# A planned attention and state-space kernel: a planner that counts semaphore waits, more plans to choose from, and eleven more slots for exp results

## The chip, the cores and the metric

The kernel runs on one core of a Trainium2 chip. The metric is the time of one execution on the device in microseconds (us). The engines of the core are TensorE (PE in the profile; PEld are its weight loads), VectorE (DVE), ScalarE (ACT), GpSimd (POOL) and SyncE (SP), which issues most of the DMAs. Each engine has its own stream of instructions in a fixed order, and they wait for one another by semaphores.

## What is computed

Two independent parts, whose outputs lie side by side. Part A is a state-space layer over 2048 steps with 640 states. Part B is attention with 32 heads that share one key and one value head, over 2048 positions.

```python
def _A_ref(x, Lambda_re, Lambda_im, B_re, B_im, C_re, C_im, log_dt, Dskip):
    ...                                   # Lam_bar, B_bar from Lambda, log_dt, B
    Bu = jnp.einsum("bld,pd->blp", x + 0j, B_bar)
    for t in range(L):
        h = Lam_bar[None, :] * h + Bu[:, t, :]
        hs.append(h)
    return 2.0 * jnp.einsum("blp,dp->bld", hseq, Cmat).real + x * Dskip[None, None, :]

def _B_ref(x, wq, wk, wv, wo):            # S = 2048, D = 640, H = 32, Dh = 20
    q = ...                               # x @ wq, in 32 heads
    k, v = x @ wk, x @ wv                 # one head
    p = _softmax(jnp.einsum("bhqd,bkd->bhqk", q, k) * (Dh ** -0.5))
    o = jnp.einsum("bhqk,bkd->bhqd", p, v)
    return ... @ wo
```

The exponentials are the bulk: 32 heads x 2048 x 2048. The kernel cuts them into 2048 tiles of 128 keys x 512 queries; 64 tiles are a block (four heads, 512 queries, all keys).

## The kernel before

The kernel is not written instruction by instruction. A planner runs when it is built: operations with an engine, a planned duration, dependencies and a priority go through a small event model of the engines, and whichever operation an engine would take next is appended to the program. The order is fixed then. On the chip nothing of the plan's times is left; only the order of each engine and the semaphore waits are.

```python
class Schedule:
    OUT = {"pe": 200.0, "act": 130.0, "dve": 110.0, "pool": 150.0, "dma": 60.0}  # ns until another engine sees a result
    ...
    def begin(self, op, eng):
        ...
        if op.dma_key is not None:
            self.free[eng] = self.t + op.tail * len(op.fns)
            ...
        else:
            op.end = self.t + op.dur + op.tail
            self.free[eng] = self.t + op.dur - (self.EARLIER.get(eng, 0.0) if op.psum else 0.0)
        self.order.append(op)
```

Several plans are made, with task times shaken by a seed, and the one whose last operation ends first in the model is kept:

```python
    PLANS = 24
    def planned(self):
        for seed in range(self.PLANS):
            ...
            plan.s.run()
            end = max(op.end for op in plan.s.order)
            if best is None or end < best[0]:
                best = (end, plan)
```

A tile of scores is made by one matmul from KT and QT into one of eight 512-column PSUM banks. There are two ways from scores to exponentials.

The ScalarE way: one ACTIVATE turns two or three banks at once (SC0 or SC1, 1024 or 1536 columns) into bf16 in slots of PR, and one matmul for each tile multiplies it by the values (VP), accumulating in the bank MB3. There are 24 slots:

```python
    NPT = 24
    def fill(self, op, i):
        ...
        h = self.pr_take(n)
        ...
        dst = p.PR[:, h.index:h.index + n, :]
        ex = self.act(lambda e: e.activation(dst, t[:, 0:512 * n], ACT.Exp, scale=1.0 / UNIT), 0.8333 * 512 * n + 64, ...,
                      gate=lambda: all(x.taken and x.left == 0 and self.s.done(x.users) for x in h.prev))
```

The VectorE way: a first step adds a constant to the scores and writes integers whose bits are a coarse bf16 exponential; three more copies with other shifts (VectorE or GpSimd, two tiles at a time) are made from it; all four are multiplied by scaled values (VS) and summed by TensorE, so such a tile costs four matmuls. The results are the slots DR: 20 of their own at first and 21 more (MORE) once the space of x, wq and QP, all in one tensor BIG, is no longer needed.

```python
    NDS = 20
    MORE = 21
        first = self.dve(self.ts(self.dr(h.index), bank.ap, 16256.0, 0.0, ALU.add, ALU.max), 645, ...)   # in fill_d
            op.fns.append(self.ts(at(dst), at(src), float(self.SHIFTS[k][0]), 0.0, ALU.add, ALU.max))    # in copy
```

How many tiles go which way is not fixed: up to a share of 0.265 a tile goes the VectorE way whenever a bank, enough free DR slots and VectorE's state in the model allow it. All other tasks (projections of q, the state-space units, the output products) are fitted between.

At the start TensorE runs dummy matmuls on zeros while it has nothing else, so that its clock is up when work comes; the planner takes them for 260 ns each. When work runs low later, short dummy matmuls (KT, VZ) do the same.

```python
    def warm_source(self):
        ...
        return Op("pe", [self.mm(self.pvbank.ap, p.PR[:, 0, 0:128], p.PR[:, 0, :], True, True)], 260.0, prio=9, ...)
```

In the profile L1218 is the ACTIVATE of exps, L652 the additions of the VectorE way, L647 among others GpSimd's copies, L637 and L633 the matmuls.

Of the kernel before, what the change touches and what calls it, by code (L numbers as in the profile page):

```python
# [22 lines left out]
class Op:  # L23


    __slots__ = ("eng", "fns", "dur", "deps", "prio", "reads", "writes", "prev", "gate", "hook", "start", "end",
                 "seq", "land", "dma_key", "idx", "tail", "mode", "load", "late", "port", "after", "due", "table", "psum")

    def __init__(self, eng, fns, dur, deps=(), prio=5, reads=(), writes=(), prev=None, gate=None, hook=None,
                 dma_key=None, land=0.0, tail=0.0, mode="F", load=0.0, port=False):  # L30
        self.eng, self.fns, self.dur = eng, list(fns), dur
        self.deps, self.prio, self.prev = list(deps), prio, prev
        self.reads, self.writes = list(reads), list(writes)
        self.gate, self.hook = gate, hook
        self.dma_key, self.land, self.tail = dma_key, land, tail
        self.mode, self.load, self.late = mode, load, False
        self.port, self.after, self.due, self.table = port, [], None, None
        self.psum = any(k[0] == "B" and k[1:].isdigit() for k in self.reads)
        self.start = self.end = None
        self.seq = self.idx = 0  # L40


class Schedule:
# [3 lines left out]


    ENGINES = ("pe", "act", "dve", "pool", "sp")
    OUT = {"pe": 200.0, "act": 130.0, "dve": 110.0, "pool": 150.0, "dma": 60.0}  # L50
    OWN = {"pe": 0.0, "act": 60.0, "dve": 115.0, "pool": 100.0}
    URGENT = 1.0

# [8 lines left out]
    def __init__(self, seed=0):  # L62
        self.rng = random.Random(seed) if seed else None
        self.t = 0.0
        self.pending = {e: [] for e in self.ENGINES}
        self.free = {e: 0.0 for e in self.ENGINES}
        self.order = []
        self.events = []
        self.procs = []
        self.dma_free = {}  # L70
        self.n = 0
        self.mode = None
        self.late_from = 0.0
        self.loads = []
        self.sources = {e: [] for e in self.ENGINES}
        self.slack = {"pe": 60.0, "dve": 150.0}
        self.port_free = {"dve": 0.0, "pool": 0.0}
        self.port_last = {"dve": None, "pool": None}
        self.port_wanted = False
        self.pipe, self.table = 0.0, None  # L80

    def recent(self, span):

# [44 lines left out]
    def begin(self, op, eng):  # L128
        if op.hook is not None:
            op.hook(op)  # L130
        op.start = self.t
        if op.late:
            self.late_from = self.t + op.dur + self.PAUSE
        if eng == "pe":
            if op.mode != self.mode:
                op.dur += self.SWITCH
                self.mode = op.mode
            self.loads.append((self.t, op.load))
        if op.port:
            if eng == "pool" and self.port_last["dve"] is not None:  # L140
                op.after.append(self.port_last["dve"])
            self.port_free[eng] = self.t + op.dur + (self.LOCK if eng == "pool" else 0.0)
            self.port_last[eng] = op
            self.at(self.port_free[eng])
        if op.dma_key is not None:
            self.free[eng] = self.t + op.tail * len(op.fns)
            s = max(self.t + 1300.0, self.dma_free.get(eng, 0.0), self.pipe)
            self.dma_free[eng] = self.pipe = s + op.dur
            op.end = max(s + op.dur + 700.0, self.free[eng] + 1700.0) + op.land
        else:  # L150
            if op.table is not None and op.table != self.table:
                self.table = op.table
                op.dur += self.TABLE
            op.end = self.t + op.dur + op.tail
            self.free[eng] = self.t + op.dur - (self.EARLIER.get(eng, 0.0) if op.psum else 0.0)
        self.order.append(op)
        self.at(self.free[eng])
        for lag in (0.0, 60.0, 100.0, 110.0, 115.0, 130.0, 150.0, 200.0):
            self.at(op.end + lag)

    stay = staticmethod(lambda: True)

# [252 lines left out]
class Build:  # L415
# [3 lines left out]
    NOP = 7  # L419
    NRD = 3  # L420
    NDS = 20
    MORE = 21
    SHARE = 0.265

    SHIFTS = ((0, 0.2421875), (32, 0.201171875), (64, 0.169921875), (96, 0.142578125))
# [13 lines left out]
    def build(self):  # L439
        nc = self.nc  # L440
        with ExitStack() as o:
            self.banks = []
            self.slots = []
            sizes = list(self.CHUNKS) + [1] * (8 - sum(self.CHUNKS))
            self.psum = [o.enter_context(nc.psum_tensor(f"{'SC' if i < len(self.CHUNKS) else 'MB'}{i}", [128, 512 * n], FP32))
                         for i, n in enumerate(sizes)]
            self.alloc(o)
            base = nc.sbuf_bytes_remaining
            with ExitStack() as p1:
                self.alloc_early(p1)  # L450
                early = base - nc.sbuf_bytes_remaining
            with ExitStack() as p2:
                self.alloc_late(p2)
                late = base - nc.sbuf_bytes_remaining
                if late < early:
                    self.sb(p2, "pad", [128, (early - late) // 4 + 8], FP32)
                plan = self.planned()
                shares = {k: self.EARLY for k in self.LATE}
                shares.update({k: self.EARLY for k in ("pb0", "pb1", "lb", "qt")})
                shares.update({f"W{c}_0": self.EARLY + ["pb0", "pb1"] for c in range(NC)})  # L460
                shares.update({f"W{c}_1": self.EARLY + ["lb", "qt", "pc0", "pc1"] for c in range(NC)})
                shares.update({"pc0": ["lb"], "pc1": ["qt"]})
                shares.update({f"CB{c}": [f"xbT{i}_{k}" for i in range(2) for k in range(NC)] for c in range(NC)})
                shares.update({f"CT{tb}_{c}": [f"xn{tb}"] for tb in range(2) for c in range(NC)})
                shares.update({f"DR{self.NDS + i}": over for i, over in enumerate(self.dr_over)})
                shares["WOt"] = [f"BT{i}_{c}" for i in range(2) for c in range(NC)]
                shares.update({f"OPT{k}": [f"BA{i}_{c}" for i in range(2) for c in range(NC)] for k in self.EARLY_O})
                em = Emitter(nc, plan.s.order, [b.key for b in plan.banks], shares)
                em.plan()
                with nc.Block() as block:  # L470
                    em.emit(block)
# [15 lines left out]
        self.early = [b for b in self.banks if b not in rest]  # L487

    SPREAD = 12.0
    PLANS = 24  # L490

    def planned(self):

        best = None
        for seed in range(self.PLANS):
# [3 lines left out]
            try:  # L499
                plan.s.run()  # L500
            except RuntimeError:
                continue
            end = max(op.end for op in plan.s.order)
            if best is None or end < best[0]:
                best = (end, plan)
        return best[1]
# [1 line left out]
    def alloc(self, o):  # L508
# [9 lines left out]
        for c in range(NC):  # L518
            for m in range(2):
                self.dr_at.append(2048 * c + 640 + 512 * m)  # L520
                self.dr_over.append([f"xbT{i}_{c}" for i in (1, 2, 3)])
        for m in range(6):
            self.dr_at.append(ends[0] + 512 * m)
            self.dr_over.append(["wqa", "wqb"])
        for m in range(NC):
            self.dr_at.append(ends[1] + 512 * m)
            self.dr_over.append([f"QP{m}"])
        self.xaT = sb(o, "xaT", [128, NC, 2, 512], BF16)
        self.BT = sb(o, "BT", [128, 2, NC, 640], BF16)
        self.BA = sb(o, "BA", [128, 2, NC, 640], BF16)  # L530
# [124 lines left out]
    def program(self):  # L655
# [9 lines left out]
        self.q_op, self.qd_op, self.half_op, self.scat_op, self.rd_op, self.brow_op = {}, {}, {}, {}, {}, {}  # L665
        self.o_ops, self.y_ops, self.w_op, self.xa_op = {}, {}, {}, {}
        self.state_op = {}
        self.owner = [None] * self.NPT
        self.pr_at = 0
        self.waiting = []  # L670
        self.dhold = [Holder(i) for i in range(self.NDS)]
# [28 lines left out]
    def warm_source(self):  # L700
# [4 lines left out]
        if self.started:  # L705
            if self.s.recent(3000.0) > self.WARM:
# [1 line left out]
            fns = self.four(self.pvbank, [p.VZ[:]] * 4, p.KT[:, 0:512], True, True)  # L708
            return Op("pe", fns, self.mmt(512), prio=3.5, mode="C", load=512.0, reads=["VZ", "KT0"], writes=[self.pvbank.key],
                      deps=[self.c_op["VZ"], self.kt_op[0]])  # L710
        return Op("pe", [self.mm(self.pvbank.ap, p.PR[:, 0, 0:128], p.PR[:, 0, :], True, True)], 260.0, prio=9,
                  load=512.0, deps=[self.zero_op], reads=["PR0"], writes=[self.pvbank.key], hook=self.warm_last)

    WARM = 4500.0
    V_AT, BOUND_AT = (-88, -87), -99

# [467 lines left out]
    def fill(self, op, i):  # L1184
# [16 lines left out]
        ents = []  # L1201
        for x, m in enumerate(tiles):
            b, kc, j = self.score(op, m, t[:, 512 * x:512 * x + 512], banks[x])
            ents.append((b, kc, j, p.PR[:, h.index + x, :]))
        first = [] if own is None else [self.fill_d(op, own, banks[2])]
        if first:
            other = self.slot_last[1 - i][0]
# [6 lines left out]
        op.reads = sorted(set(op.reads))  # L1214
        op.dur = self.mmt(512, len(op.fns))
        op.load = 128.0 * len(op.fns)
        dst = p.PR[:, h.index:h.index + n, :]
        ex = self.act(lambda e: e.activation(dst, t[:, 0:512 * n], ACT.Exp, scale=1.0 / UNIT),  # L1218
                      0.8333 * 512 * n + 64, table="exp",
                      deps=[op], reads=[b.key for b in banks[:n]], writes=keys, prio=0.5,  # L1220
# [32 lines left out]
        return h  # L1253

    def pr_next(self, n):
        return self.pr_at if self.pr_at + n <= self.NPT else 0

    def tight(self):

# [171 lines left out]
    def more(self):  # L1431

        yield lambda: NQB - 1 in self.row_mm and self.s.done([self.row_mm[NQB - 1]]) \
            and all(self.s.done([self.qd_op[NQB - 1, i]]) for i in range(NC))
        self.dhold += [Holder(self.NDS + i) for i in range(self.MORE)]

    def d_free(self):

# [865 lines left out]
```

## Time and profile before

| | |
|---|---|
| median of 3 runs | 745.45 us (744.23 to 745.55) |
| span of the profiled execution | 743.5 us |
| exps on ScalarE | 676 instructions, 475 of two tiles and 201 of three: 1553 tiles |
| first steps of the VectorE way | 456 from SC banks and 39 from MB banks: 495 tiles |
| GpSimd copies | 401 |

The page has the busy time of each engine, the span in 40 slices with the busy share of each in tenths, and the chain of waits followed back from the last instruction. A group line has the engine, the operation, output and input, shape and count; then its busy time and the mean duration of one, then the idle time of the engine before it and who ended it. Busy time counts overlaps of following instructions once, the mean does not. A timeline line merges instructions that follow each other on an engine: start, length, engine, line, the shape of the first, and how many.

### The profile page before, as it was taken

What the parts mean: (1) busy time and instruction counts of PE and PEld (TensorE: products, weight loads), DVE (VectorE), ACT (ScalarE), POOL (GpSimd) and SP (SyncE); (2) the same over time, 40 slices, a digit from 0 to 9 for tenths busy, and PEclk for the clock granted to TensorE, in tenths of its full rate; (3) what the DMA queues carried; (4) which work ended last, traced back from release to release, by engine and by line L of the source; (5) the groups of instructions that cost most, each with busy time, mean ns of one, the idle gap of its engine ahead of it and who ended that gap; (6) DMA issues with size and microseconds to landing.
All of it is one profiled execution on the core that took longest, in us unless ns stands there. A gap on an engine that the chain in (4) does not pass through costs nothing.

```text
span 743.5 us, 26647 instructions
## 1 busy us (share of the span) xinstructions
PE 711.7 (96%) x11323; PEld 255.9 (34%) x11323; DVE 665.3 (89%) x1367; ACT 722.9 (97%) x702; POOL 426.3 (57%) x448
## 2 busy tenths in 40 slices
PE   9999899998999999999999999989999999999997
PEld 3422222234443533332333333323333333332332
DVE  6888999989788798999898999998998998988995
ACT  5999999999999999999999999999999999999995
POOL 3766566430266558367476674566754835778460
PEclk9999999999999999999999999998999999999999
DMA  9414443364220100101100000110000011100101
GB/s 200 70 41 129 91 113 90 89 144 78 48 60 10 25 20 21 51 11 35 42 26 23 17 30 19 40 46 19 19 14 19 9 27 30 37 16 17 26 14 37
DMA packets 78089, 34.43 MB, mean 46 GB/s; under 512 B 58852, under 2 KB 77972, under 8 KB 77972
## 3 DMA queue, kind: packets, MB, share of 16 engines
q1 hardware_dynamic: 76352, 32.34, 18.3%
q8 instruction: 90, 1.47, 0.8%
q10 hardware_dynamic: 1620, 0.39, 0.3%
q14 instruction: 27, 0.22, 0.1%
HBM read 11.53 MB, written 9.75 MB: 29 GB/s over the span
## 4 chain that ended last, share of the span: by engine, by line
ACT 59%; PE 34%; DVE 6%; issue 1%; DVEq 0%
ACT PR L1218 59%; PE MB L637 12%; PE SC L637 11%; PE MB L633 10%; DVE BIG L652 2%; DVE prod L647 1%; DVE W L652 1%; DVE CT L647 1%; DVE CA L647 1%; DVE g L2046 0%; PE SC L633 0%; DVE pvsb L1580 0%; DVE CT L651 0%; DVE CA L651 0%; PE SC L935 0%
## 5 line engine op out<-in xcount | busy, mean ns | idle before, releaser
L1218 ACT ACTIVATE PR<-SC 128x1024 bf16<-128x1024 f32 (+1 forms) x676 | 708.6, 1252 | 3.3 <-PE SC L637 2.1
L647 POOL TENSOR_TENSOR BIG<-BIG,step 128x512 int32<-128x512 int32 x401 | 407.4, 1045 | 286.1 <-DVE BIG L652 163.1
L652 DVE TENSOR_SCALAR BIG<-SC 128x512 int16<-128x512 f32 x456 | 302.8, 684 | 38.5 <-PE SC L637 34.9
L637 PE MATMUL SC<-QT,KT 32*128 32x512 bf16 x2009 | 265.3, 386 | 23.0 <-ACT PR L1218 16.0
L637 PE MATMUL MB<-BIG,VS 128*32 128x512 bf16 x1980 | 248.5, 386 | 1.2 <-issue 0.6
L637 PE MATMUL MB<-PR,VP 128*32 128x512 bf16 x1553 | 217.4, 386 | 0.8 <-DVE pvsb L1580 0.6
L637 PEld LDWEIGHTS SC<-QT,KT 32*128 32x128 bf16 x2009 | 67.8, 91 | 258.2 <-ACT PR L1218 165.3
L652 DVE TENSOR_SCALAR BIG<-BIG 128x1024 int16<-128x1024 int16 (+1 forms) x356 | 129.0, 419 | 8.6 <-PE MB L637 7.0
L637 PEld LDWEIGHTS MB<-BIG,VS 128*32 128x32 bf16 x1980 | 62.6, 95 | 66.7 <-issue 44.1
L637 PEld LDWEIGHTS MB<-PR,VP 128*32 128x32 bf16 x1553 | 53.5, 94 | 54.6 <-issue 41.0
L633 PE MATMUL MB<-CT,W 128*32 128x320 bf16 (+2 forms) x1040 | 49.7, 301 | 0.2 <-DVE BIG L2006 0.2
L633 PE MATMUL MB<-xaT,BT 128*32 128x256 bf16 x800 | 34.5, 274 | 0.0
L633 PE MATMUL MB<-xaT,BA 128*32 128x256 bf16 x800 | 33.6, 274 | 0.1
L633 PE MATMUL MB<-CA,W 128*32 128x512 bf16 (+1 forms) x640 | 31.2, 301 | 0.1
L647 DVE TENSOR_TENSOR prod<-MB,tab 128x1024 bf16<-128x1024 f32 x20 | 24.3, 1215 | 3.7 <-PE MB L633 3.7
L652 DVE TENSOR_SCALAR BIG<-MB 128x512 int16<-128x512 f32 x39 | 26.5, 680 | 1.1 <-PE MB L637 0.7
L633 PEld LDWEIGHTS MB<-CT,W 128*32 128x32 bf16 x1040 | 21.4, 96 | 17.0 <-issue 7.9
L633 PE MATMUL MB<-WO,OP 128*32 128x128 bf16 (+1 forms) x576 | 26.5, 297 | 0.1
L1761 DVE CAST stg<-MB 128x512 bf16<-128x512 f32 x35 | 23.9, 683 | 2.6 <-PE MB L633 2.3
L633 PE MATMUL MB<-BIG 128*32 128x512 bf16 x340 | 25.6, 383 | 0.0
L2046 DVE TENSOR_TENSOR_SCAN g<-sc,hst,prod 128x256 bf16<-128x256 f32 x30 | 23.1, 776 | 0.0
L633 PEld LDWEIGHTS MB<-xaT,BA 128*32 128x32 bf16 x800 | 19.0, 96 | 9.0 <-issue 5.4
(167 smaller groups left out, 421.2 us busy)
## 6 DMA issues: line engine op xcount, KB each, us to landing
out_dram<-stg SPq DMA_DIRECT2D x31, 128.0 KB, 1.7
qd<-BIG SPq DMA_DIRECT2D x20, 128.0 KB, 1.8
QT<-qd SPq DMA_DIRECT2D x28, 80.0 KB
OP<-pvsb SPq DMA_DIRECT2D x105, 20.0 KB
rdP<-recs SPq DMA_DIRECT2D x105, 20.0 KB
W<-in_A_B_re_dram SPq DMA_DIRECT2D x10, 160.0 KB, 2.7
W<-in_A_B_im_dram SPq DMA_DIRECT2D x10, 160.0 KB, 2.7
lbd<-W SPq DMA_DIRECT2D x10, 160.0 KB, 2.0
```

The lines of the kernel that those rows point to most:

```text
L633: r = e.matmul(out[32 * j:32 * j + 32], lhsT=lhsT[:, 32 * j:32 * j + 32], rhs=rhs, start=start, stop=stop, tile_position=(0, 32 * j), skip ...
L637: return lambda e: e.matmul(out, lhsT=lhsT, rhs=rhs, start=start, stop=stop, **kw)
L647: return lambda e: e.tensor_tensor(out, a, b, op)
L652: return lambda e: e.tensor_scalar(out, a, s1, s2, op0=op0, op1=op1)
L1218: ex = self.act(lambda e: e.activation(dst, t[:, 0:512 * n], ACT.Exp, scale=1.0 / UNIT), 0.8333 * 512 * n + 64, table="exp", deps=[op], re ...
L1761: ev = self.dve(lambda e: e.tensor_copy(st, bank.ap), 645, deps=[prev], reads=[bank.key], writes=[key], prio=self.EV, gate=(lambda: last.e ...
L2046: o = self.dve(lambda e, ri=ri, init=init: e.tensor_tensor_scan(p.g[:, u, ri, :], rdec, p.prod[:, 1, 0, ri, :], init, ALU.mult, ALU.add), ...
```

## The change

Four things. (1) In the planner's model an operation that starts before its inputs are seen by the engine keeps the engine until they are; until now waits that the emitted program has, but that the planner's list of dependencies lacked (a buffer to be read before it is overwritten, a bank that another engine reads), took no time in the model. A result of ScalarE is seen after 225 ns instead of 130. A cold dummy matmul is planned at 450 ns. (2) Each finished plan is replayed in order, with each operation starting when its engine is free and all that it waits for is seen (215 ns after TensorE), and the plan with the earliest end of that replay is kept. (3) 40 plans instead of 24. (4) The last eleven of the 21 late slots of the VectorE way become slots for exps ("wide"), so that there are 35 late on instead of 24, and 30 slots for the VectorE way instead of 41.

```diff
-    OUT = {"pe": 200.0, "act": 130.0, "dve": 110.0, "pool": 150.0, "dma": 60.0}
+    OUT = {"pe": 200.0, "act": 225.0, "dve": 110.0, "pool": 150.0, "dma": 60.0}
+    SEEN = {"pe": 215.0, "act": 225.0, "dve": 110.0, "pool": 150.0, "dma": 60.0}
...
+    def stall(self, op):
+        eng, late = op.eng, self.t
+        found = list(op.after)
+        for k in op.reads:
+            if k in self.writer:
+                found.append(self.writer[k])
+            if k[0] == "B" and k[1:].isdigit():
+                found += [x for x in self.readers.get(k, ()) if x.eng != eng]
+        for k in op.writes:
+            if k in self.writer:
+                found.append(self.writer[k])
+            found += self.readers.get(k, ())
+        op.found = [d for d in found if d is not op and (eng != "pe" or d.eng != "pe")]
+        for d in op.found:
+            late = max(late, self.seen(d, eng))
+        ...
+        return late - self.t
...
+        wait = self.stall(op)
+        if wait > 0.0:
+            if op.dma_key is None:
+                op.dur += wait
+                op.stall = wait
...
+    def replayed(self):
+        ...
+        for op in self.order:
+            e = op.eng
+            t = free[e]
+            for d in op.found:
+                out = self.SEEN["dma"] if d.dma_key is not None else self.OWN.get(e, 0.0) if d.eng == e else self.SEEN[d.eng]
+                t = max(t, end[id(d)] + out)
+            dur = op.dur - op.stall
+            ...
+        return max(end.values())
...
-    MORE = 21
+    MORE = 10
...
-    PLANS = 24
+    PLANS = 40
...
-            end = max(op.end for op in plan.s.order)
+            end = plan.s.replayed()
...
-        for m in range(6):
-            self.dr_at.append(ends[0] + 512 * m)
-            self.dr_over.append(["wqa", "wqb"])
-        for m in range(NC):
-            self.dr_at.append(ends[1] + 512 * m)
-            self.dr_over.append([f"QP{m}"])
+        self.wide_at = [(self.NPT, 6, ends[0]), (self.NPT + 6, NC, ends[1])]
+        self.pr_over = [["wqa", "wqb"]] * 6 + [[f"QP{m}"] for m in range(NC)]
...
-        return Op("pe", [...], 260.0, prio=9,
+        return Op("pe", [...], self.COLD if self.s.t < self.WARMED else 240.0, prio=9,
...
+    COLD, WARMED = 450.0, 6000.0
...
-        dst = p.PR[:, h.index:h.index + n, :]
+        dst = self.pr(h.index, n)
...
     def pr_next(self, n):
-        return self.pr_at if self.pr_at + n <= self.NPT else 0
+        ends = [self.NPT] + ([at + k for at, k, _ in self.wide_at] if self.wide else [])
+        ...
...
         self.dhold += [Holder(self.NDS + i) for i in range(self.MORE)]
+        self.wide = True
```

## The prediction

> **What bounds the kernel now.** I read the page first, for the share of each engine:
>
> ```profile
> PE 711.7 (96%) x11323; PEld 255.9 (34%) x11323; DVE 665.3 (89%) x1367; ACT 722.9 (97%) x702; POOL 426.3 (57%) x448
> ACT  5999999999999999999999999999999999999995
> PEclk9999999999999999999999999998999999999999
> ACT 59%; PE 34%; DVE 6%; issue 1%; DVEq 0%
> ```
>
> ScalarE (ACT) is busy 97% of the span, and the two slices in which it is not are the first and the last. The chain of waits leaves ScalarE for 41% of the span, but that alone doesn't say that ScalarE waits: a chain also goes through a matmul that ended just as the exp before it did. So I asked how fast exps can follow each other. The groups by shape give the counts, the timeline of ScalarE gives stretches that are nearly of one shape (start, length, engine, line, form of the first, count of all):
>
> ```profile
> L1218 ACT ACTIVATE PR<-SC 128x1024 bf16<-128x1024 f32 x475 | 447.9, 1112 | 2.0 <-PE SC L637 1.4
> L1218 ACT ACTIVATE PR<-SC 128x1536 bf16<-128x1536 f32 x201 | 277.9, 1585 | 1.3 <-PE SC L637 0.7 <-PE MB L637 0.4
> ```
>
> ```profile
> 152.67 39.65 ACT L1218 ACTIVATE PR<-SC 128x1024 bf16<-128x1024 f32 x30
> ...
> 659.53 28.48 ACT L1218 ACTIVATE PR<-SC 128x1536 bf16<-128x1536 f32 x30
> ...
> 324.76 1.02 ACT L1218 ACTIVATE PR<-SC 128x1024 bf16<-128x1024 f32 x1 [0.29 <-PE SC L637]
> ...
> 733.23 1.19 ACT L1218 ACTIVATE PR<-SC 128x1024 bf16<-128x1024 f32 x1
> ```
>
> In the trace's records the first stretch is 2 exps of two tiles and 28 of three (all of three from 153.58), the second the reverse. The means 1112 and 1585 ns overlap from one exp to the next, so they are not costs. Call S and L what a two-tile and a three-tile exp add. The exp that stands alone took 1.02, some 0.1 over S, so a stretch has 0.1 of latency: 2S + 28L = 39.55 and 28S + 2L = 28.38. The difference gives L - S = 11.17/26 = 0.430, the sum L + S = 67.93/30 = 2.264: **S = 0.917 us, L = 1.347 us**, and a tile more costs 0.430.
>
> All exps of the kernel before then need 475 x 0.917 + 201 x 1.347 = 435.6 + 270.7 = 706.3 us. They run from 23.02 to 734.42 (733.23 + 1.19), which is 711.4. So the kernel before is **23.0 us of start, 706.3 us of exp work, 5.1 us of stalls between exps, and 9.1 us of tail**. That sum is what the change can act on. Everything else is hidden behind ScalarE.
>
> **What the Trainium skill says.** "ScalarE: Activation LUTs", section "What ACT_TABLE_LOAD costs", gives 186 ns + 0.833 ns per element for an ACTIVATE and some 93 ns of overlap with the next; an estimate from it is 0.946 us for 1024 elements and 1.373 us for 1536. The trace agrees on the slope (0.430 us for 512 elements against 0.427) and is about 30 ns lower on the fixed part; I take the trace. "Perfetto Trace Analysis", section "Identifying the Most-Contended Engine", says that matmul busy time is no measure of how near TensorE is to its limit and that for ScalarE occupancy is. This trace agrees: PE shows 96% with weight loads at 34%, and exps still follow each other nearly without a gap. "TensorE: Matmul & The Clock Gate", Part 1, says that a 512-column matmul takes 426.7 ns while the array is cold and 215.7 ns once warm; nine warm-up matmuls that end just before 9.4 (below) stand 0.216 apart, and the first five near 0.43, so the trace agrees. That is what the new figure COLD = 450 is for.
>
> **The change part by part.**
>
> (1) *The planner charges waits to the engine.* An operation whose inputs aren't seen yet keeps its engine for that long, and a result of ScalarE is seen after 225 ns instead of 130. No duration on the chip changes; what changes is the order, and with it how many tiles go the VectorE way. Counted in the two programs: the VectorE way makes 482 tiles instead of 495 (first steps 428 + 54 against 456 + 39; matmuls with VS 1928 against 1980, four per tile). ScalarE therefore makes 1566 tiles instead of 1553, in 448 two-tile exps, 223 three-tile ones and one of a single tile. With S and L: 448 x 0.917 + 223 x 1.347 + 0.49 (S less 0.430) = 410.8 + 300.4 + 0.5 = 711.7, against 706.3: **+5.4 us on the bounding engine**. The 13 fewer first steps at the 684 ns of that group give VectorE some 9 us, GpSimd has 21 fewer copies; neither is the bound, so this pays only through fewer stalls.
>
> (2) *Fewer warm-up matmuls at the start.* The timeline of TensorE, before:
>
> ```profile
> 5.83 0.19 PE L637 MATMUL MB<-ident,vrow 20*128 20x20 bf16 x1
> 5.96 1.03 PE L637 MATMUL MB<-PR 128*128 128x512 bf16 x2
> 6.92 0.62 PE L637 MATMUL MB<-PR,VZ 128*32 128x512 bf16 x4
> 7.47 2.12 PE L637 MATMUL MB<-PR 128*128 128x512 bf16 x9
> 9.44 1.06 PE L637 MATMUL SC<-ident,CT 128*128 128x128 bf16 x16
> 10.51 0.40 PE L637 MATMUL MB<-BIG 128*20 128x512 bf16 x4
> ```
>
> The first part of x (read as CT) had landed at 6.06 by its semaphore, the second at 8.61, yet the transposes began at 9.44: they stood behind warm-up matmuls that were planned at 260 ns and took some 430 while cold. The new program has 3 + 2 + 1 + 6 of them ahead of the transposes instead of 5 + 4 + 2 + 9, eight fewer. The transposes can begin about 1.9 us earlier. But the four matmuls after them need the first part of wq, which landed at 9.33, so only 10.51 - 9.45 = 1.06 us get through, and later steps (table tiles on ScalarE before its exp table load, five warm-ups instead of three before the bound) eat some of it. I take **-0.8 us** for the first exp.
>
> (3) *40 plans instead of 24, judged by an in-order replay with 215 ns after TensorE, and eleven slots more for exps* (24 + 11, ten instead of 21 spare slots for VectorE's tiles). This acts on the 5.1 us of stalls and on nothing else in the middle. The stalls come in knots; the largest, by the chain of waits and the windows:
>
> ```profile
> 494.51 4.33 DVE BIG L652 x11
> 498.85 0.66 DVE g L2046
> 499.51 1.18 DVE BIG L652 x2
> ...
> 500.00:600.00 100.00, 95.28 (x1602) 35.91 (x1606) 91.67 (x176) 98.71 (x95) 62.50 (x62) 0.97 0.07 18
> ```
>
> At the end of a block TensorE waited for eleven copies of VectorE, its granted clock then halved for 6.8 us (0.97 in that window), and ScalarE stood. More room for exps lets the next block go on meanwhile, and a VectorE with 13 tiles less reaches the end of a block sooner. I expect two thirds of the stalls to go: **-3.3 us**.
>
> (4) *The tail.* The new program's last VectorE steps are 9 copies after the last bank copy but one, with twelve keep-warm matmuls among the last attention matmuls; before it was similar with none. **+0.3 us**.
>
> Sum: 5.4 - 0.8 - 3.3 + 0.3 = +1.6 us on 745.45: **747.0 us**.
>
> **The rivals.**
> *Stalls were larger than the page shows, and the new model removes them.* If the 41% of the chain off ScalarE were true waiting, a faithful plan could win tens of us. For it: the weight loads for scores wait 165 us for exps in the list of waits. Against it: those are TensorE's waits, and the sum above has room for 5.1 us only. Even with no stall at all and 1.2 us off the start the time would be 745.45 + 5.4 - 5.1 - 1.2 = 744.6.
> *The model is now too timid.* Charging waits makes the planner hand VectorE less than it can do (it is 89% busy), ScalarE pays 5.4 us, and the stalls, being 0.7% already, hardly shrink: 745.45 + 5.4 - 0.8 - 0.5 + 0.5 = 750.
> *The halved pool of spare slots for VectorE's tiles becomes a wait of its own:* copies have nowhere to go, blocks end late and TensorE's clock halves more often. Each such knot cost some 1.5 us before; four more of them would give 753. Against it: the planner sees the slots and the number of tiles fell by 13 only.
>
> **Range and chances.** The exp count is certain, so the range is that of stalls and start: 744.0 (nothing left of the stalls) to 751.0 (stalls unchanged or slightly worse). 2% is 14.9 us: faster by that is out of reach, since the exp work with start and tail alone is above it (1%); slower needs 13 us of new stalls beyond the sum (2.5%).
>
> **What would show it.** In the changed profile: exps x448, x223 and x1 by shape (their lines are split between PR and BIG); first exp near 22.2; last exp's end less first start near 713.5, so stalls near 2; no stretch of half clock or fewer; PE's transposes from about 7.5. I'm wrong if S or L differ for exps written to BIG, if the first exp comes at 23 or later, or if the stretch of exps exceeds 717.

## The result and the profile after

The changed kernel takes 751.3 us (median of 4 runs, 749.59 to 753.57) where the kernel before took 745.1 beside it: a ratio of 1.0087, 95% interval 1.0058 to 1.0116. Six more runs of it in a later batch gave 750.5 (ratio 1.0062, 1.0039 to 1.0086; the ratios come from all single times, so they aren't exactly the quotients of the medians). By the 2% measure this is "same". It is a small loss all the same: the predicted 747.0 was 4.3 us too low, and the upper end of the predicted range, 751.0, was 0.3 us too low.

The page of the changed kernel: busy time by engine, two rows of the slices, the chain.

```profile
PE 711.8 (95%) x11258; PEld 255.7 (34%) x11259; DVE 654.0 (87%) x1361; ACT 727.9 (97%) x698; POOL 406.1 (54%) x427
...
ACT  5899999999999999999999999999999999999995
...
PEclk9899999999999999999999999999999999999999
...
ACT 77%; PE 14%; SPq 2%; DVE 2%; DMA 2%; issue 1%; POOL 0%; DVEq 0%
```

ScalarE (ACT) has 5 us more of busy time, VectorE 11 us less, GpSimd 20 us less. The chain stays on ScalarE for 77% of the span instead of 59%: the chain is cleaner, the time longer. Slice 2, whole before, now has a dip in both rows; that is new.

The groups of ScalarE by shape (count | busy us, mean ns | idle before):

```profile
L1272 ACT ACTIVATE PR<-SC 128x1024 bf16<-128x1024 f32 x351 | 334.9, 1116 | 3.6 <-PE SC L689 2.3 <-PE MB L689 0.9
L1272 ACT ACTIVATE PR<-SC 128x1536 bf16<-128x1536 f32 x169 | 237.3, 1589 | 1.8 <-PE SC L689 1.8
L1272 ACT ACTIVATE BIG<-SC 128x1024 bf16<-128x1024 f32 x97 | 95.1, 1112 | 0.2 <-PE SC L689 0.2
L1272 ACT ACTIVATE BIG<-SC 128x1536 bf16<-128x1536 f32 x54 | 77.4, 1572 | 0.0
```

351 + 97 = 448 two-tile exps and 169 + 54 = 223 three-tile ones, as counted. The means are near those of the kernel before (1112 and 1585 ns), but means overlap from one exp to the next. What counts is the time from the end of one exp to the end of the next where ScalarE doesn't wait between them. Its median in this trace is 0.917 us for two tiles and 1.343 us for three, the same to PR and to BIG and the same as in the kernel before. So S and L hold, writing to the new slots costs nothing extra, and the exp work is 711.7 us.

The start, in TensorE's timeline (start, length, then idle before it and who ended it):

```profile
7.76 1.06 PE L689 MATMUL SC<-ident,CT 128*128 128x128 bf16 x16
8.66 0.38 PE L689 MATMUL MB<-PR 128*128 128x512 bf16 x1
9.55 0.40 PE L689 MATMUL MB<-BIG 128*20 128x512 bf16 x4 [0.51 <-DMA BIG<-in_B_wq_dram]
```

The transposes begin at 7.76 instead of 9.44, and TensorE then waits for the first part of wq, which landed at 9.41. ScalarE's timeline after that, and its first stretch of the kernel before:

```profile
22.44 7.41 ACT L1272 ACTIVATE PR<-SC 128x1024 bf16<-128x1024 f32 x8
30.23 1.02 ACT L1272 ACTIVATE PR<-SC 128x1024 bf16<-128x1024 f32 x1 [0.38 <-PE SC L689]
31.55 1.02 ACT L1272 ACTIVATE PR<-SC 128x1024 bf16<-128x1024 f32 x1 [0.30 <-PE SC L689]
33.50 1.02 ACT L1272 ACTIVATE PR<-SC 128x1024 bf16<-128x1024 f32 x1 [0.93 <-PE MB L689]
35.01 1.94 ACT L1272 ACTIVATE PR<-SC 128x1024 bf16<-128x1024 f32 x2 [0.48 <-PE SC L689]
```

```profile
23.02 13.86 ACT L1218 ACTIVATE PR<-SC 128x1024 bf16<-128x1024 f32 x15 [0.58 <-PE SC L637]
```

The first exp comes 0.58 us earlier (22.44 against 23.02). Before, 15 exps then follow each other without a gap; after, ScalarE stands four times and 2.1 us in all. The windows of after around that place (length, then busy us and count of PE, PEld, DVE, ACT, POOL, then TensorE's granted clock), and two windows of before:

```profile
24.70:28.10 3.40, 2.78 (x39) 1.93 (x36) 3.24 (x13) 3.40 (x5) 3.06 (x8) 1.00 0.50 113
28.10:31.50 3.40, 3.40 (x27) 0.79 (x31) 2.86 (x13) 2.77 (x3) 3.03 (x7) 0.50 0.19 41
31.50:34.90 3.40, 3.40 (x28) 0.59 (x27) 1.69 (x4) 2.05 (x2) 2.11 (x6) 0.50 0.02 5
34.90:38.30 3.40, 3.40 (x49) 0.91 (x47) 2.55 (x5) 3.27 (x4) 1.64 (x2) 0.99 0.13 44
```

```profile
28.10:31.50 3.40, 3.24 (x50) 1.33 (x49) 3.06 (x11) 3.40 (x5) 2.98 (x7) 1.00 0.17 39
31.50:34.90 3.40, 3.40 (x49) 1.00 (x50) 2.27 (x5) 3.40 (x5) 1.92 (x5) 1.00 0.02 5
```

For 6.8 us the clock is 0.50, TensorE gets 27 and 28 matmuls through in a window instead of 50 and 49, and ScalarE, fed by it, is busy 2.77 and 2.05 of 3.40 us. PE itself shows 100%: a busy share doesn't tell a slow engine from a full one.

A second place is near 170 us. The timeline of all engines there: a weight transpose and the store of a row of q (qd), both issued by SyncE, and what waits for the store:

```profile
165.62 1.14 SPq L674 DMA_TRANSPOSE BA<-lbd  x1
...
167.41 0.43 SPq L1098 DMA_DIRECT2D qd<-BIG  x1
...
169.26 0.29 DVE L703 TENSOR_SCALAR BIG<-BIG 128x512 int16<-128x512 int16 x1 [0.94 <-DMA qd<-BIG]
...
169.93 0.68 DVE L1096 CAST BIG<-MB 128x512 bf16<-128x512 f32 x1
...
170.67 0.40 PE L685 MATMUL MB<-BIG 128*32 128x512 bf16 x4 [1.30 <-DVE BIG L1096]
...
171.44 5.51 ACT L1272 ACTIVATE PR<-SC 128x1536 bf16<-128x1536 f32 x4 [0.64 <-PE SC L689]
...
175.03 0.62 DVE L703 TENSOR_SCALAR BIG<-BIG 128x512 int16<-128x512 int16 x2 [1.46 <-DMA qd<-BIG]
```

Read from the bottom of a chain: ScalarE waits 0.64 us for scores, TensorE stood 1.30 us for a bank copy, VectorE made that copy late because an absolute value ahead of it in its fixed order waited 0.94 us for a store. With a second such case at 178 us this is 1.8 us.

The knot that I had named, with its half clock from 502.5 us, is gone from that place. But the clock halves for 3.4 us at 550.4, and in the window from 500 to 600 ScalarE is nearly as idle as before (98.96 us busy against 98.71):

```profile
500.00:600.00 100.00, 93.91 (x1519) 34.39 (x1511) 94.07 (x192) 98.96 (x95) 54.61 (x53) 0.98 0.08 19
```

In the second profile of the same program it halves for 3.4 us at 119.7 us instead, and not at 550, so this fall isn't tied to its place in the order.

Sums as in the prediction (first exp, exp work with S and L, stalls as the rest of the stretch, tail), each from one profiled execution. The stretch of exps ends with these lines, first in the profile of after, then in its second profile (a_again below):

```profile
734.29 7.34 ACT L1272 ACTIVATE PR<-SC 128x1536 bf16<-128x1536 f32 x6
```

```profile
732.44 7.34 ACT L1272 ACTIVATE PR<-SC 128x1536 bf16<-128x1536 f32 x6
```

| us | first exp | exp work | stalls | tail | span |
|---|---|---|---|---|---|
| before | 23.0 | 706.3 | 5.1 | 9.1 | 743.5 |
| after | 22.4 | 711.7 | 7.5 | 10.2 | 751.8 |
| after, second profile | 22.4 | 711.7 | 5.7 | 10.3 | 750.1 |

The stretch is 741.63 - 22.44 = 719.2 us and in the second profile 717.4, both past the 717 that the prediction named as a sign of being wrong. 5.4 us of the loss is exp work. The stalls, which were to shrink by 3.3, are 0.6 to 2.4 us larger.

### The profile page after: what moved, and what is told of

Read it like the earlier page. It is cut to its first block, busy times and chain, and to the rows that moved or that the text cites. A ratio compares the mean times of both kernels' runs of the same rounds, so it can differ in the third digit from the quotient of the medians.

```text
span 751.8 us, 26430 instructions
## 1 busy us (share of the span) xinstructions
PE 711.8 (95%) x11258; PEld 255.7 (34%) x11259; DVE 654.0 (87%) x1361; ACT 727.9 (97%) x698; POOL 406.1 (54%) x427
## 4 chain that ended last, share of the span: by engine, by line
ACT 77%; PE 14%; SPq 2%; DVE 2%; DMA 2%; issue 1%; POOL 0%; DVEq 0%
ACT PR L1272 58%; ACT BIG L1272 19%; PE SC L689 5%; PE MB L685 4%; PE MB L689 4%; SPq L674 2%; PE SC L685 1%; DVE BIG L704 1%; DMA BIG<-in_B_x_dram 1%; DMA qd<-BIG 1%; DMA rdP<-recs 0%; POOL BIG L699 0%; DVE BIG L1096 0%; SPq L670 0%; DVE PR L699 0%
## 5 line engine op out<-in xcount | busy, mean ns | idle before, releaser
L1272 ACT ACTIVATE PR<-SC 128x1024 bf16<-128x1024 f32 (+1 forms) x521 | 559.2, 1268 | 5.4 <-PE SC L689 4.1
L699 POOL TENSOR_TENSOR BIG<-BIG,step 128x512 int32<-128x512 int32 x380 | 387.4, 1048 | 312.9 <-DVE BIG L704 171.8
L704 DVE TENSOR_SCALAR BIG<-SC 128x512 int16<-128x512 f32 x428 | 284.9, 685 | 46.8 <-PE SC L689 43.2
L689 PE MATMUL MB<-BIG,VS 128*32 128x512 bf16 x1928 | 214.7, 383 | 1.9 <-DVE BIG L704 0.9
L1272 ACT ACTIVATE BIG<-SC 128x1024 bf16<-128x1024 f32 (+1 forms) x151 | 170.1, 1276 | 0.2 <-PE SC L689 0.2
L689 PE MATMUL MB<-PR,VP 128*32 128x512 bf16 x1210 | 155.2, 387 | 0.3 <-ACT BIG L1272 0.3
L689 PEld LDWEIGHTS MB<-BIG,VS 128*32 128x32 bf16 x1928 | 54.5, 95 | 63.7 <-issue 35.8
L689 PE MATMUL MB<-BIG,VP 128*32 128x512 bf16 x356 | 54.4, 384 | 0.0
L689 PEld LDWEIGHTS MB<-PR,VP 128*32 128x32 bf16 x1210 | 38.9, 94 | 42.1 <-issue 32.6
L704 DVE TENSOR_SCALAR BIG<-MB 128x512 int16<-128x512 f32 x54 | 36.8, 681 | 3.2 <-PE MB L689 3.2
```

The costliest lines, as they stand in the source:

```text
L689: return lambda e: e.matmul(out, lhsT=lhsT, rhs=rhs, start=start, stop=stop, **kw)
L699: return lambda e: e.tensor_tensor(out, a, b, op)
L704: return lambda e: e.tensor_scalar(out, a, s1, s2, op0=op0, op1=op1)
```

## The experiments

Three theories, which the experiments were to tell apart. *The parts:* ScalarE's 13 extra tiles are the loss, and undoing the part that costs them, the charged waits or the slots, gives its share back. *The places:* the two new knots, the clock's fall near 28 us first of all, are the loss, and taking them out gives it back. *The draw:* the stalls belong to no part of the change; they come with whatever order the planner happens to keep (the draw), and the kernel before is a good draw. (Letters in the expectations are those of each batch.)

**What needed no chip.** With the old rule for the kept plan (latest end) instead of the replay, the program built is the same, instruction for instruction. With 24 plans instead of 40, again the same. Parts (2) and (3) of the change therefore do nothing here: seed 20 is kept by either rule. Over all 40 seeds the changed planner gives 475 to 484 tiles to VectorE, the old one 489 to 496. The 13 lost tiles are the rule, not the seed. Slots undone alone gives 8 of them back, charging undone alone 6, both 13.

**Undoing parts.**

```diff
# a_slots: the eleven wide slots are VectorE's again
-    MORE = 10
+    MORE = 21
...
# a_nocharge: waits not charged to the engine
-                op.dur += wait
-                op.stall = wait
+                pass
# a_slots_nocharge: both.  a_again: the changed kernel as it is
```

> The changed kernel once more, for its spread and a second profile. Theory (exp work): the exps start near 22.4, their work is 711.7 us again, so about 751 us with 7 to 10 us of stalls. Rival (one bad execution was profiled): 748 or less, with stalls under 5 us.

> The changed kernel with the eleven wide slots given back to VectorE's tiles (MORE 21). Counted in the program: 490 tiles of VectorE instead of 482, exp work 708.5 us by S and L instead of 711.7. Theory (the slots cost tiles and tiles cost ScalarE time): 3.2 us less than the changed kernel, 748.1. Rival 1 (slots matter to the stalls, exp slots were worth having): no gain or a loss, 751 or more. Rival 2 (all of the loss is the planner's charging of waits): 751.

> The changed kernel without the charging of waits to an engine in the plan; slots, replay and 225 ns stay. 488 tiles of VectorE, exp work 709.2 us. Theory (tiles): 2.5 us less than the changed kernel, 748.8, stalls alike. Rival (charging makes the order fit the chip): the stalls grow by more than 2.5 us, 751 or more.

> Both undone; the ScalarE delay of 225 ns, the replay, 40 plans and the cold figure stay. 495 tiles of VectorE, exp work 706.3 us as in the kernel before. Theory (tiles): 5.4 us less than the changed kernel, 745.9, so the kernel before within 1.5 us. Rival (stalls and tail of the new order are the loss): 748.5 or more, since only the tile count goes back.

| | median us | ratio to before (interval) | exp work | stalls in profile (one execution) |
|---|---|---|---|---|
| a_again | 750.5 | 1.0062 (1.0039 to 1.0086) | 711.7 | 5.7 |
| a_slots | 750.72 | 1.0059 (1.0039 to 1.0079) | 708.5 | 8.0 |
| a_nocharge | 750.41 | 1.0061 (1.0041 to 1.0081) | 709.2 | 6.1 |
| a_slots_nocharge | 749.87 | 1.0063 (1.0041 to 1.0085) | 706.3 | 8.5 |

The exp work falls exactly as the tiles come back, by up to 5.4 us, and the time by 0.6. The groups of a_slots_nocharge show that its work is that of the kernel before (470 and 204 exps, and one of one tile), with more idle time on the two-tile ones:

```profile
L1276 ACT ACTIVATE PR<-SC 128x1024 bf16<-128x1024 f32 x470 | 444.1, 1113 | 6.8 <-PE SC L693 5.7 <-PE MB L693 0.4
L1276 ACT ACTIVATE PR<-SC 128x1536 bf16<-128x1536 f32 x204 | 281.9, 1581 | 0.0
```

By the theory of the parts each should have given its share back. None did. (In a_nocharge a DMA that waits still holds its queue in the plan; 225 ns, COLD and 40 plans stay in all of them.) Net, the eleven slots neither gain nor cost anything that can be measured. One could read the table as slots that pay back in stalls what they cost in tiles; but the redraws that follow move the stalls as far without any slot, so that reading isn't shown.

**Doing one part on the kernel before, or only drawing again.**

```diff
# b_p40: the old planner, 40 plans (another seed is kept)
-    PLANS = 24
+    PLANS = 40
# b_seed0: the old planner, only the plan that isn't shaken
-    PLANS = 24
+    PLANS = 1
# b_out225: ScalarE seen after 225 ns, with the matching event time
-    OUT = {"pe": 200.0, "act": 130.0, ...
+    OUT = {"pe": 200.0, "act": 225.0, ...
# b_cold: only the dummies of the start planned at 450 ns
-        return Op("pe", [...], 260.0, prio=9,
+        return Op("pe", [...], 450.0 if self.s.t < 6000.0 else 240.0, prio=9,
# b_share482 (later batch): as few tiles for VectorE as after, by the share alone
-    SHARE = 0.265
+    SHARE = 0.2402
```

> The kernel before with 40 plans instead of 24 and nothing else; another plan is kept (496 tiles of VectorE, exp work 705.9 us, 0.4 less than before). Theory A (the order of the kernel before is a lucky draw, and any redraw from the same planner has 3 or more us of stalls more): 748 to 750, stalls 9 to 11 us. Theory B (the 225 ns of ScalarE make TensorE take other work before scores, and that costs the stalls): as before, 745. Theory C (tiles on ScalarE alone): 744.7.

> The kernel before with the unshaken plan only (PLANS = 1): 496 tiles of VectorE, exp work 705.9 us. Theory A (luck of the draw): 747 to 751, stalls 8 to 12 us. Theories B and C: 745 within 1 us.

> The kernel before with ScalarE's results seen after 225 ns instead of 130, and nothing else: 492 tiles, exp work 707.5 us. Theory B: 749 to 751, with more waits of ScalarE for scores spread over the whole span. Theory A: 748 to 750 too, but with the stalls in a few knots. Theory C: 746.3.

> The kernel before with cold dummy matmuls planned at 450 ns, and nothing else; the start and with it all later order is redrawn: 495 tiles, exp work 706.3 us as before. First exp near 22.4 in all theories (0.6 us gained). Theory A: 747 to 750 all the same, stalls 9 or more. Theories B and C: 744.5.

> The kernel before with VectorE's share lowered from 0.265 to 0.2402, so that it gets 482 tiles as in the changed kernel; exp work 711.8 us instead of 706.3. Theory of the prediction (tiles on ScalarE are paid in full, stalls as in any redraw 7 to 10): 750 to 752. Theory D (ScalarE on one side and VectorE with TensorE on the other bound the kernel together, so a tile moved is paid back in fewer stalls): 746 to 748, stalls 2 to 4.

| | median us | ratio to before (interval) | exp work against before | time less exp work, against before |
|---|---|---|---|---|
| b_p40 | 744.34 | 1.0006 (0.9994 to 1.0017) | -0.4 | +0.3 |
| b_seed0 | 748.28 | 1.0054 (1.0040 to 1.0068) | -0.4 | +4.2 |
| b_out225 | 748.24 | 1.0060 (1.0035 to 1.0086) | +1.2 | +2.6 |
| b_cold | 747.25 | 1.0036 (1.0019 to 1.0054) | 0.0 | +2.8 |
| b_share482 | 749.41 | 1.0058 (1.0042 to 1.0074) | +5.5 | -0.9 |

(The last column is the difference of the medians less the column before it; before was 744.48 in the first four and 744.84 in the last.)

b_share482 is the cleanest measure of the tiles: the old planner, the old slots, 482 tiles on VectorE. Its groups of exps,

```profile
L1218 ACT ACTIVATE PR<-SC 128x1024 bf16<-128x1024 f32 x454 | 428.8, 1136 | 2.6 <-PE SC L637 2.3
L1218 ACT ACTIVATE PR<-SC 128x1536 bf16<-128x1536 f32 x219 | 303.7, 1603 | 0.5 <-PE SC L637 0.4
```

with one exp of a single tile make 454 x 0.917 + 219 x 1.347 + 0.49 = 711.8 us of work, and it is 4.6 us slower than before. So here the tiles are paid nearly in full. It is one plan, and its order is new too: its profile has 3.1 us of stalls, 2.0 less than before, as theory D of its expectation said, while its time lies between the two theories (750 to 752, 746 to 748). b_seed0 shows the other half: the same planner, nearly the same work, only another seed, and 3.8 us more. A new order alone moved the time by -0.1 us (b_p40, where theory A had expected 748 to 750) or by 3.8, which is the theory of the draw. That draw isn't wholly blind: when the programs are built, the planner's own end is 737.0 us for the plan of before, 736.8 for b_p40 and 738.6 for b_seed0. In b_out225 theory B wanted waits spread over the whole span. Its profile, taken of its longest run (753.86), has them in knots, where the clock is half for 27 us in all between the first exp and the last. No run undid the 225 ns on the changed kernel, so a share of theirs in its loss isn't excluded.

**Keeping the clock up.** Eight groups (seven in b_cold_keep) of four short dummy matmuls with zeros as weights (256 columns) among the thin work between 24 and 29 us; in a_keepabs the absolute values of the q rows also stand behind the bank copy that they held up near 170 us.

```diff
# a_keep; b_cold_keep: the same on b_cold
+        more = [plan.mm(bank.tensor[32 * j:32 * j + 32, bank.off:bank.off + 256], plan.VZ[:], plan.KT[:, 0:256], ...) for j in range(4)]
+        for o in order[first:last]:
+            if o.eng == "pe" and ("pick" in o.reads or "wvr" in o.reads):
+                o.fns = more + o.fns
...
# a_keepabs: as a_keep, and each absolute value of q moves behind the copy two blocks on
+                    order.insert(j, order.pop(i))
```

> The changed kernel, same order of everything, with one quad of 256-column dummy matmuls put ahead of each small matmul (the bound's and the values') of the first ten score groups: 8 quads between 24 and 29 us. Theory E (TensorE has too little to do there, its clock halves near 28 for 6.8 us and ScalarE stalls 2.4 to 2.7 us): the clock stays full, those stalls shrink to under 0.5, 2 us less than the changed kernel, 748.8. Rival (the clock's fall there doesn't follow that window's load): the fall stays, 750.8. Rival (scores wait behind the dummies): stalls of another kind in the same place, 750 or more.

> As a_keep, and besides VectorE's absolute values of q, which wait for the store of q to land, stand behind the bank copy after the next in VectorE's order instead of ahead of it. Theory (VectorE, and behind it TensorE, stood for those stores near 170 to 178): the 2.0 us of stalls there go, where they occur; half to 2 us less than a_keep, 747 to 748. Rival (that knot comes and goes with the DMA queues): no difference to a_keep within 0.7 us.

> The kernel before with cold dummies planned at 450 ns and the same 7 quads of dummy matmuls between 24 and 29 us. Theory E (b_cold's slower runs are those whose clock halves near 28): the spread of b_cold's times shrinks, median 744.0, 0.5 to 1 us below the kernel before as its first exp comes 0.6 us sooner. Rival: as b_cold, 747 with the same spread.

Measured: a_keep 752.9 (ratio 1.0094, 1.0065 to 1.0123), a_keepabs 753.24 (1.0100, 1.0071 to 1.0128), b_cold_keep 749.06 (1.0050, 1.0031 to 1.0068). None is faster than its kernel without the dummies (750.5 and 747.25, other batches), as the theory of the places would need. The windows of a_keepabs around its fall:

```profile
25.70:29.10 3.40, 3.40 (x43) 1.94 (x42) 2.25 (x9) 3.05 (x4) 3.08 (x7) 1.00 0.49 111
29.10:32.50 3.40, 3.40 (x35) 1.02 (x34) 2.06 (x8) 1.75 (x3) 2.71 (x7) 0.50 0.04 10
32.50:35.90 3.40, 3.40 (x34) 0.86 (x30) 1.34 (x5) 2.17 (x3) 1.63 (x4) 0.50 0.00 0
35.90:39.30 3.40, 3.40 (x29) 0.64 (x25) 2.05 (x4) 2.42 (x3) 0.00 (x0) 0.50 0.11 39
```

In the window ahead of the fall TensorE is now busy all 3.40 us (and 3.37 in the one before that), and the clock falls all the same, for three windows instead of two. The opposite is found in b_cold, whose profile has no fall near there, with TensorE hardly busier than in after (2.82 us against 2.78):

```profile
24.70:28.10 3.40, 2.82 (x37) 1.79 (x34) 3.33 (x15) 3.40 (x5) 3.05 (x7) 1.00 0.51 114
28.10:31.50 3.40, 3.40 (x50) 1.19 (x51) 2.05 (x10) 3.40 (x5) 2.95 (x8) 1.00 0.19 43
```

So idle time in TensorE's records doesn't tell whether the clock falls, and the dummies only cost. The knot at 170 us did go from the profile of a_keepabs, and the time didn't follow; in the second profile of the unchanged after it isn't there either (20 exps in a row across it): it comes in one of the two executions.

**Lump or spread.** One thing sets the new order apart at that place: the projection of q for the second head group runs as one lump of 16 matmuls at 22.6 us, where before it stood in groups of 4, 8 and 8 between scores, to 26.9 us. So I moved it, both ways; in a_spread its eviction, absolute value and bound follow it.

```diff
# a_spread: on after, one group of four after each of the next scores; b_lump: on before, all groups at the place of the first
+        for n in range(1, 5):
+            order.remove(pj[n])
+            order.insert(order.index(sc[n - 1]) + 1, pj[n])      # b_lump: order.index(pj[n - 1]) + 1
...
# a_spreadabs: a_spread, and the absolute values as in a_keepabs
# a_cold260: after, with COLD undone
-        return Op("pe", [...], self.COLD if self.s.t < self.WARMED else 240.0, prio=9,
+        return Op("pe", [...], 260.0, prio=9,
```

> Program after, with nothing changed but the place of five groups of matmuls: the projection of the second head group, which stands as one lump of 16 matmuls (22.6 to 23.6 us) behind the second pair of scores, is spread so that one group of four follows each of the next five score pairs, as the kernel before has it; its eviction, absolute value and bound follow it. Exp work as in after (710.0 us). Theory A (the lump leaves TensorE with thin work from 24.4 to 28 us, and that halves its clock near 28 us): no half clock between 25 and 38 us, stalls 2.0 to 2.7 us smaller, about 748.5 us. Rival B (the clock falls there by something else, such as fewer warming matmuls, or from execution to execution): the half clock is still there, time 750 to 752.

> The kernel before, with the same projection drawn together into one lump of 20 matmuls at its first place (24.7 us), nothing else moved. Theory A: the clock now halves near 28 us here too, and the time rises by 2 to 2.7 us, to about 747. Rival B: 744.5 to 745.5, no half clock between 25 and 38 us.

> After with the warming load of the start put back to 260 (26 warming matmuls before the first scores instead of 18); the order afterwards is the same but for a few steps. Theory A (lump): no change, half clock near 28 us stays, 750 to 751.5. Rival C (the missing warming matmuls let the clock fall): no half clock near 28 us, 748 to 749.

> Spread projection as in a_spread, and the absolute values of the later query rows stand behind the bank copy that they held up near 170 us. If both knots are what after has too much, stalls fall from 7.4 to 9.2 us to about 4 and the time is 746.5 to 747.5; if another wait takes their place, it stays at 748.5 or above.

| | median us | ratio to before (interval) | clock halved near 30 us, in the profile |
|---|---|---|---|
| a_spread | 752.42 | 1.0103 (1.0084 to 1.0122) | from 29.7, 6.8 us |
| b_lump | 746.58 | 1.0028 (1.0018 to 1.0039) | from 28.7, 10.2 us |
| a_cold260 | 751.43 | 1.0092 (1.0069 to 1.0114) | from 31.5, 3.4 us |
| a_spreadabs | 752.15 | 1.0103 (1.0082 to 1.0123) | from 31.1, 3.4 us |

b_lump did what theory A of this batch said: nothing but the place of sixteen matmuls changed, the time rose by 2.0 us, and its profile has the fall. It isn't there in every execution: of the 22 runs, 744.7 to 749.5, seven have a mean granted clock of 0.997 or more, while 10.2 us at half clock alone take 0.007 off the mean. The windows:

```profile
25.30:28.70 3.40, 1.97 (x26) 0.89 (x22) 2.68 (x10) 2.97 (x4) 3.09 (x7) 1.00 0.44 98
28.70:32.10 3.40, 3.40 (x33) 0.96 (x33) 1.83 (x5) 3.04 (x4) 2.10 (x5) 0.51 0.19 43
32.10:35.50 3.40, 3.40 (x34) 0.85 (x30) 0.93 (x2) 2.18 (x3) 1.64 (x4) 0.50 0.00 0
```

But a_spread, the other way round, kept the fall and gained nothing: the lump is enough to bring the fall on in the kernel before, and not what after has it from. Nor is it the missing warm-up matmuls: a_cold260 has them all and its clock still falls; its first exp came at 23.73 instead of 22.44, so in the profiles COLD is worth 1.3 us at the start of after, which the median (751.43 against 750.5) shows only in part. What decides whether the clock falls there in after stays open. No version beat both kernels; b_p40 is level with before.

**Times at like clock.** Each execution has a mean granted clock of TensorE beside its time, and the two go together. In the 129 executions of the kernel before in these four batches the clock lies between 0.981 and 1.000, and 0.001 less goes with 0.43 us more (correlation -0.92); in the 22 of b_cold with 0.52 us (-0.99). So kernels can be compared among executions of like clock (median us, executions):

| clock | before | b_p40 | b_cold | b_lump | b_share482 | after and a_again |
|---|---|---|---|---|---|---|
| 0.997 or more | 744.3 (69) | 744.1 (13) | 744.3 (7) | 745.2 (7) | 748.6 (7) | none |
| 0.991 to 0.994 | 746.0 (24) | 745.4 (2) | 747.9 (4) | 747.5 (7) | 750.3 (4) | 751.0 (10) |

With the clock up, b_cold loses nothing: the 2.8 us of its median come with the clock's falls. b_share482 keeps 4.3 us of its 5.5 us of tiles at full clock, and after has 5.0 us more than before at the same clock, where the exp work says 5.4. So the tiles are most of the loss, and a lower clock (median 0.992, where before has 0.997) adds to it. It also hides part of what a_slots_nocharge gave back: its median clock is 0.989, against 0.995 for before beside it, an estimated 2.6 us (6 x 0.43) of its 4.8. Why a_slots gained nothing, at the clock of a_again (both 0.9925) and with 3.2 us less work, stays open. This is a comparison and not an experiment; no run set the clock.

## Why the prediction was wrong

**The failed step is (3)**: "I expect two thirds of the stalls to go: -3.3 us". They didn't go: in the profiles they are 0.6 and 2.4 us larger (5.7 and 7.5 against 5.1). Three things in that step were wrong.

First, its means. The replay and the sixteen more plans keep the very plan that the old rule keeps, which the two built programs show. I could have asked that before predicting.

Second, its cause. I took the stalls for a want of slots and for late ends of blocks, because the largest knot looked like that. a_slots shows that the slots are worth nothing measurable in sum. The larger knots in the profiles of after are falls of TensorE's clock and, in one of two executions of after, a late store. The planned time of a matmul doesn't depend on the clock, neither in the model nor in its replay, so neither can see such a fall. The Trainium skill, "TensorE: Matmul & The Clock Gate", Part 1, says that the clock is set by a monitor that watches a free-running window of 3413 ns and that where it switches is different from run to run. These traces agree in the lengths: the falls that begin between 26.9 and 31.5 us last 3.4, 6.8 or 10.2 us, in every profile that has one. The page ties the fall to an idle window. Here the measurement differs, as far as the trace tells busy from idle: the clock of a_keepabs fell after a window in which TensorE's records are busy throughout.

Third, its sign for a new order. The kernel before is a good draw. Of the changes that left it the same or nearly the same work, b_p40 cost nothing, b_lump 2.0 us, b_cold 2.8, b_out225 2.6 and b_seed0 4.2 beyond their work, and none gained; b_share482 alone had 0.9 us less than its work. Part of these figures is the clock of the executions (all of it in b_cold). That a new order from a better model should have fewer stalls was hope; the default should have been the same or a little more. With 0 in place of -3.3 the sum is 750.3, where the two medians are 751.3 and 750.5. (That the kernel before was chosen among many by its measured time is argued from this, not shown.)

**(1), the exp work, +5.4, was right**: counts, S, L and the writes to BIG all came out as worked out, and b_share482 moved the same number of tiles without the rest and lost 4.6 us (4.3 at full clock).

**(2), the start, -0.8, was right in mechanism and a little large**: -0.58, with the transposes at 7.76 and the wait for wq as foreseen.

**(4), the tail, +0.3, was too small**: +1.1 in the profile. The last stores carry it. DMA issues of after, then of before (count, KB each, us to landing):

```profile
out_dram<-PR SPq DMA_DIRECT2D x3, 128.0 KB, 2.9
out_dram<-PR ACTq DMA_DIRECT2D x2, 128.0 KB, 2.5
```

```profile
out_dram<-PR SPq DMA_DIRECT2D x3, 128.0 KB, 2.0
out_dram<-PR ACTq DMA_DIRECT2D x2, 128.0 KB, 2.1
```

From the last addition or copy before a store to the end of the span, after needs 4.4 us (751.8 less 747.36) and before 3.5 (743.5 less 739.98). No run was made on the cause. With the same order at the end a_keep and a_keepabs had a tail of 9.5, and the other four profiles of that order 10.3 or 10.4.

**The rivals.** "The model is now too timid", with 750, came nearest, for the reason it gave: ScalarE pays for the tiles and the stalls hardly shrink. That large hidden stalls would vanish is refuted by the sum. That the halved pool would become a wait finds no support: a_slots gave the slots back and gained nothing.

## What to carry to other kernels

When stalls are 1% of a kernel's time, more work for its bounding engine is a sure loss and fewer stalls are an uncertain gain: count the bound's instructions in the new program first, and give expected gains on stalls no credit until the program shows which wait is gone. Redraw the order with nothing else changed (another seed) before reading a difference of half a per cent as the effect of a change: here such redraws moved the time by -0.1 to +3.8 us. Compare executions of like clock where the clock is known: b_cold, 2.8 us behind by its median, is level with before there. And test by building whether a new criterion picks another plan at all.

## What the runs showed of the hardware

TensorE's clock fell to half while its records showed it 58%, 82% or 100% busy in the 3.4 us before (b_lump, after, a_keepabs), and dummy matmuls with zero weights of 32 columns in between didn't prevent that. In the 129 executions of the kernel before, 0.001 less of mean clock goes with 0.43 us more of about 745. Such a fall can cost ScalarE, the bound, a good 2 us: a score matmul pair took 0.60 us instead of 0.39, and feeding an exp then takes longer than the exp (they started 1.3 to 2.0 us apart, where S is 0.917).
